# The order of all steps between up-projections given by tables per block, y summed by halves, decode scratch in other places

## The chip, the core and the metric

The kernel runs on one core of one Trainium2 chip. TensorE multiplies into PSUM banks, VectorE and ScalarE read those banks and work on SBUF, POOL (GpSimd) works on SBUF alone, and SyncE issues nearly all transfers. Each engine runs its own instructions strictly in the order of the program; between engines there are semaphores. The metric is the device time of the whole program in microseconds, as the median of several executions.

## What is computed

A Mamba2 scan over chunks (the kernel takes chunks of 128 tokens), and then a maxout feed-forward on its output:

```
# per batch b and head h, chunk by chunk (cum: running sum of log a in the chunk)
M       = (C @ B.T) * exp(cum_i - cum_j) * causal
y       = M @ x + (C @ state) * exp(cum_i)
state   = exp(cum_last) * state + sum_j B_j x_j exp(cum_last - cum_j)
...
# y as (3072 tokens, 256) = (batch * seq, heads * head_dim)
h   = max(y @ w1, y @ w2, y @ w3)          # 768 hidden values
out = h @ w_out                            # 256
```

The shapes are x (4, 8, 768, 32), B and C (4, 8, 768, 16), w1 to w3 (256, 768) and w_out (768, 256). The weights are float64 and are decoded in the kernel.

## The kernel before, in words

The sequence has six blocks of 128 tokens (NC = 6); one block holds 4 batches, so 512 tokens. Each block runs through the scan and then through the feed-forward, and the two are interleaved: while the feed-forward of block c runs on TensorE, the scan of block n = c + 1 is worked off between its matmuls.

The scan of a block n: B and C are transposed (`scan_b`, `scan_tc`), ScalarE masks C into even and odd heads (`scan_c`), E holds the decays (`scan_e` takes their exponential, `scan_cd` on VectorE multiplies them into C: Cd). `scores` makes four banks of scores for two batches, and four steps of `scan_weight` (L566) multiply them on VectorE with the decay matrix L, whose exponentials ScalarE makes in eight parts of four (`part`, `decay_part`, L459) after POOL has masked L (`decay_masks`, L452). `scan_old` multiplies the state with Cd (L581, four row groups of the array), `scan_own` adds the product of the weighted scores with x (L594); both sum into the two banks of y. `scan_y` makes of y its high part `hi` on ScalarE (L621), and `lo` and the difference `d` on VectorE (L622, L629). `scan_state` makes the state for the next block.

The feed-forward of a block c > 0 is a line of 18 units (nine weight matrices k, halves g): a unit opens a bank with two matmuls of `d` (`unit_open`, L699, the delta matmuls), ScalarE scales the bank by a constant (`down_scaled`, L685), four matmuls of the high and low parts follow (`unit`, L716), and VectorE copies the bank into m or takes the maximum (L721, L723). The banks of the units form a ring of four, and openings run up to three units ahead. Every third matrix completes a hidden row f: `hidden` makes its high part on ScalarE (L635) and then its low part and difference on VectorE (L638, L629). `down_next` issues the down product of a block in four pieces; L763 is that of block 0, L768 that of the others, where the pieces Y take the differences and X the other parts. `put` scales the result and sends it out.

Block 0 has plain float32 up-projections (18 steps n, L655), and in the steps between them the weights are decoded: ScalarE (L210, L219), VectorE (L211, L214), POOL (L220), and later a sign step on VectorE (L223). `split` then makes high part, low part and difference of each of the twelve weight chunks (step 0 on ScalarE, L257 and L258, steps 1 and 2 on POOL, L259 and L252). The seam between block 0 and block 1 sums y of block 1.

What stands between two units is given by lists per matrix (X1, Y1, D1, K1, W1 for block 1, X2, Y2, D2, K2 for the later ones), by `pop(2)` after each unit, which takes two steps off the list `later` (score weightings, `lo` and `d` of y, state), and by `after(1, ...)`, which puts the two parts of a hidden row one unit later each.

Of the kernel before, what the change touches and what calls it, by code (L numbers as in the profile page):

```python
# [20 lines left out]
def kernel(  # L21
# [53 lines left out]
    SMALL, LARGE = 2.0 ** -15, 122880.0 - 2.0 ** -7  # L75

# [114 lines left out]
    def decode_steps():  # L191
# [9 lines left out]
        room = six((1, 2, 5)[n % 3] if n < 10 else 2).rearrange("p (a f) -> p a f", a=2)  # L201
# [3 lines left out]
        def first():  # L205
# [3 lines left out]
            held["u"] = u = room[:, 0].bitcast(U32)  # L209
# [8 lines left out]
            r = room[:, 1].bitcast(U32)  # L218
# [23 lines left out]
    def weight_parts(k):  # L242
# [5 lines left out]

        def last():
            d = wsum.tile([P, 2, WCOL], F32R, tag="w", name="wd")  # L250
            parts[k].append(d)
            nc.gpsimd.tensor_tensor(  # L252
                out=d.rearrange("p k f -> p (k f)"), in0=hi.bitcast(FP32), in1=lo.bitcast(FP32),
                op=ALU.subtract)
# [4 lines left out]
            lambda: nc.gpsimd.tensor_tensor(  # L259
# [99 lines left out]
    Ls = {}  # L359
# [212 lines left out]
    def scan_old(c):  # L572

        st = blocks[c]
        st["y"] = ys = [att_bank([P, NB, P], "y") for _ in range(KD)]
        Sp = states[c]
        for b in range(NB):
            for r in range(NP):
                rows = slice(r * PN, (r + 1) * PN)
                q = r % 2 * 2 * D  # L580
                nc.tensor.matmul(  # L581
                    out=ys[r // 2][q:q + 2 * D, b],
                    lhsT=Sp[rows, b].rearrange("p g d -> p (g d)"), rhs=st["Cd"][rows, b],
                    start=(b == 0), stop=False, tile_position=(r * PN, q),
                    skip_group_check=True)

    def scan_own(c, bs):

        st = blocks[c]
        M = Ls[c]  # L590
        for b in bs:
            for h in range(NH):
                t, q = divmod(h, QH)
                nc.tensor.matmul(  # L594
                    out=st["y"][t][q * D:(q + 1) * D, b], lhsT=st["x"][:, b * NH + h],
                    rhs=M[:, b, h], start=False, stop=True,
                    tile_position=(0, q * D), skip_group_check=True)
# [17 lines left out]
    def scan_y(c):  # L615

        yT[c] = hi, lo, d = [
            six(3 * (c % 2) + j, F32R).rearrange("p (k t) -> p k t", k=KD) for j in range(3)]
        for t in range(KD):
            y = blocks[c]["y"][t].rearrange("p b i -> p (b i)")  # L620
            nc.scalar.activation(hi[:, t], y, AF.Copy, scale=HIGH)  # L621
            later.append(lambda t=t, y=y: nc.vector.tensor_tensor(  # L622
                out=lo[:, t], in0=y, in1=hi[:, t].bitcast(FP32), op=ALU.subtract))
            later.append(lambda t=t: difference(d[:, t], hi[:, t], lo[:, t]))
        later.append(lambda: ready.add(c))
# [41 lines left out]
    later, due = [], []  # L667
# [7 lines left out]
    def after(n, step):  # L675

        due.append((units[0] + n, step))

    def run_due():
        while due and due[0][0] <= units[0]:  # L680
            due.pop(0)[1]()
# [8 lines left out]
    AHEAD, ends = 2, []  # L690
# [13 lines left out]
    def unit():  # L704

        u = units[0]
        while len(opened) <= AHEAD and u + len(opened) < len(line) and (
                line[u + len(opened)][0] in ready):
            unit_open(u + len(opened))
        c, k, g = line[u]  # L710
        q, i = divmod(k, 3)
        o = opened.pop(u)
        cols = slice(g * P, (g + 1) * P)
        for kk in range(KD):
            for j in range(2):
                nc.tensor.matmul(  # L716
                    out=o, lhsT=weight_part(k, j, kk, cols), rhs=yT[c][j][:, kk],
                    start=False, stop=(kk == KD - 1 and j == 1), skip_group_check=True)
        if i == 0:
            m[g] = ffn.tile([P, BLK], FP32, tag="m", bufs=4, name="m")  # L720
            nc.vector.tensor_copy(out=m[g], in_=o)  # L721
        else:
            nc.vector.tensor_tensor(out=m[g], in0=m[g], in1=o, op=ALU.max)  # L723
        units[0] += 1
        run_due()
        if i == 2:
            last = c == NC - 1 and k == NW - 1

            def start(f=2 * q + g, src=m[g]):
                rest = hidden(f, src)  # L730
                if last:
                    rest()
                else:
                    after(1, rest)
            if last:
                if g == 1:
                    ends[0]()
                    start()
                else:
                    ends.append(start)  # L740
            else:
                after(1, start)
# [163 lines left out]
    signs, decodes = (0, 2, 3, 5, 7, 8, 10, 12, 14, 15, 17), (0, 2, 3, 5, 7, 8, 10, 12, 14, 15)  # L906
    W0 = {11: (0, 0), 12: (0, 1), 13: (0, 2, 1, 0), 14: (1, 1), 15: (1, 2, 2, 0), 16: (2, 1),
          17: (2, 2, 3, 0)}
    for n in range(NF * 3):
# [17 lines left out]
        if n in (13, 14, 16, 17):  # L927
            pop(2)
        if i == 0:
# [6 lines left out]
        if n in signs:  # L936
            sign()
        if n in decodes:
            decode()
        if n == 1:  # L940
            fj = from_last(R, a_sb, "fj")
        if n == 3:
# [8 lines left out]
            decay_masks(1, (0, 1))  # L951
        if n == 9:
            decay_masks(1, (2, 3))
        if n in (5, 7, 9, 11, 13, 14, 15, 16):
            part(1)
        if n == 11:
            transposed(1)
            scan_c(1)
            load(2, "C")
        if n == 12:  # L960
            scan_e(1)
            scan_cd(1)
            scores(1, 0)
        if n == 15:
            shared["att"] = False
            scores(1, 2)
        if n in W0:
            split(*W0[n])
    shared["ffn"] = False
    scan_old(1)  # L970
    scan_own(1, range(NB))
# [102 lines left out]
```

## Time and profile before

| | |
|---|---|
| time, median of 3 executions (lowest, highest) | 321.13 us (320.93, 323.64) |
| the profiled execution, whole | 320.5 us |
| its span (first to last instruction) | 318.8 us |
| mean granted clock of TensorE | 0.966 |
| busy: TensorE, VectorE, ScalarE, POOL | 279.9, 192.6, 181.9, 89.6 us |

Times in the profile are those of one execution and begin at the start of its span. "Idle before" is the time in which an engine waited before an instruction, and the name behind the arrow is what ended that wait. A granted clock of 1.00 is 2.4 GHz for TensorE, 0.5 is 1.2 GHz.

### The profile page before, as it was taken

What the parts mean: (1) busy time and instruction counts of PE and PEld (TensorE: products, weight loads), DVE (VectorE), ACT (ScalarE), POOL (GpSimd) and SP (SyncE); (2) the same over time, 40 slices, a digit from 0 to 9 for tenths busy, and PEclk for the clock granted to TensorE, in tenths of its full rate; (3) what the DMA queues carried; (4) which work ended last, traced back from release to release, by engine and by line L of the source; (5) the groups of instructions that cost most, each with busy time, mean ns of one, the idle gap of its engine ahead of it and who ended that gap; (6) DMA issues with size and microseconds to landing.
All of it is one profiled execution on the core that took longest, in us unless ns stands there. A gap on an engine that the chain in (4) does not pass through costs nothing.

```text
span 318.8 us, 5385 instructions
## 1 busy us (share of the span) xinstructions
PE 279.9 (88%) x2054; PEld 213.0 (67%) x2054; DVE 192.6 (60%) x296; ACT 181.9 (57%) x407; POOL 89.6 (28%) x84
## 2 busy tenths in 40 slices
PE   6899969599659978899997979997999997999993
PEld 4664434387438655688775868775898775797793
DVE  2767689762642468830888750888622967616662
ACT  2954977647943955923764833764844453425511
POOL 4344675759832670900021420021000000000000
PEclk9999999899957979979999999999999999999999
DMA  8979999898800359502708702800002000000001
GB/s 89 251 238 331 142 189 236 209 135 237 125 0 2 82 62 264 57 2 69 93 5 206 127 2 68 95 3 2 0 0 69 0 3 0 2 33 33 0 2 66
DMA packets 105049, 28.13 MB, mean 88 GB/s; under 512 B 75328, under 2 KB 101952, under 8 KB 105024
## 3 DMA queue, kind: packets, MB, share of 16 engines
q1 hardware_dynamic: 104720, 27.66, 42.7%
q8 instruction: 16, 0.26, 0.4%
q10 hardware_dynamic: 304, 0.13, 0.2%
q14 instruction: 9, 0.07, 0.1%
HBM read 24.54 MB, written 3.24 MB: 87 GB/s over the span
## 4 chain that ended last, share of the span: by engine, by line
PE 60%; DVE 23%; DMA 6%; ACT 4%; POOL 3%; issue 2%; SPq 0%; POOLq 0%; ACTq 0%
PE up L716 20%; PE up L699 11%; PE o L768 11%; PE s L558 5%; DVE h L629 4%; DVE h L638 4%; DMA raw_C<-in_C_dram 3%; DVE m L721 3%; PE o L763 3%; POOL six L220 3%; DVE w L223 2%; PE o L793 2%; PE y L594 2%; DMA rb<-in_moe_w_out_dram 2%; DVE six L629 2%
## 5 line engine op out<-in xcount | busy, mean ns | idle before, releaser
L716 PE MATMUL up<-six,wp 128*128 128x512 f32 x360 | 98.8, 398 | 0.0
L723 DVE TENSOR_TENSOR m<-m,up 128x512 f32<-128x512 f32 x60 | 40.9, 685 | 73.5 <-PE up L716 73.1
L685 ACT ACTIVATE up<-up 128x512 f32<-128x512 f32 x90 | 52.4, 584 | 55.9 <-PE up L699 48.6
L716 PEld LDWEIGHTS up<-six,wp 128*128 128x128 f32 x360 | 69.2, 192 | 15.5 <-ACT up L685 0.2
L699 PE MATMUL up<-six,wd 128*128 128x512 f32 x180 | 61.9, 424 | 8.0 <-DVE m L723 4.7
L459 ACT ACTIVATE L<-L,ncums 128x128 f32<-128x128 f32 x160 | 50.2, 391 | 0.9 <-POOL L L452 0.9
L699 PEld LDWEIGHTS up<-six,wd 128*128 128x128 f32 x180 | 31.6, 193 | 21.8 <-DVE m L723 7.9
L721 DVE COPY m<-up 128x512 f32<-128x512 f32 x30 | 20.6, 687 | 22.5 <-PE up L716 22.5
L566 DVE TENSOR_TENSOR L<-s,L 128x512 f32<-128x512 f32 x46 | 29.3, 682 | 0.7 <-ACT L L459 0.7
L655 PE MATMUL up<-six,w 128*128 128x512 f32 x64 | 28.8, 598 | 0.1
L558 PE MATMUL s<-six,six 32*128 32x256 f32 x192 | 20.9, 412 | 7.9 <-ACT six L500 4.0
L638 DVE TENSOR_TENSOR h<-m,h 128x512 fp32r<-128x512 f32 x30 | 26.0, 868 | 0.7 <-ACT h L635 0.7
L629 DVE SCALAR_TENSOR_TENSOR h<-h,h 128x512 fp32r<-128x512 f32 x30 | 25.4, 846 | 1.0
L452 POOL TENSOR_SCALAR_AFFINE_SELECT L<-L 128x1024 f32<-128x1024 f32 x20 | 25.4, 1292 | 0.0
L768 PE MATMUL o<-wp,h 128*128 128x256 f32 x192 | 24.3, 283 | 0.0
L768 PEld LDWEIGHTS o<-wp,h 128*128 128x128 f32 x192 | 23.9, 192 | 0.3
L558 PEld LDWEIGHTS s<-six,six 32*128 32x128 f32 x192 | 12.5, 184 | 15.3 <-ACT six L500 5.0
L545 POOL TENSOR_TENSOR S<-S,old 128x256 f32<-128x256 f32 x4 | 2.9, 734 | 69.7 <-DVE S L537 69.7
L220 POOL TENSOR_TENSOR six<-six 128x512 uint32<-128x512 uint32 x12 | 15.3, 1273 | 23.2 <-DVE six L214 16.1
L655 PEld LDWEIGHTS up<-six,w 128*128 128x128 f32 x64 | 11.8, 190 | 14.2 <-issue 11.1
L635 ACT ACTIVATE h<-m 128x512 fp32r<-128x512 f32 x30 | 18.7, 622 | 2.8 <-DVE m L723 2.7
L259 POOL TENSOR_TENSOR wp<-w,wp 128x512 fp32r<-128x512 f32 x12 | 15.4, 1284 | 15.5 <-ACT wp L257 15.5
(98 smaller groups left out, 326.2 us busy)
## 6 DMA issues: line engine op xcount, KB each, us to landing
L<-cums SPq DMA_DIRECT2D x10, 1024.0 KB, 8.8
rb<-in_moe_w_dram SPq DMA_DIRECT2D x9, 512.0 KB, 6.7
raw_x<-in_x_dram SPq DMA_DIRECT2D x6, 512.0 KB, 9.2
out_dram<-ob SPq DMA_DIRECT2D x10, 256.0 KB, 2.1
raw_B<-in_B_dram SPq DMA_DIRECT2D x6, 256.0 KB, 4.4
raw_C<-in_C_dram SPq DMA_DIRECT2D x6, 256.0 KB, 6.2
rb<-in_moe_w_out_dram SPq DMA_DIRECT2D x3, 512.0 KB, 4.8
E<-cums SPq DMA_DIRECT2D x40, 32.0 KB, 2.2
```

Of the source, the lines that this page charges most:

```text
L459: nc.scalar.activation(L[:, b, h], L[:, b, h], AF.Exp, bias=ncum[c][:, b * NH + h:b * NH + h + 1], scale=1.0)
L558: nc.tensor.matmul(out=s[:, i].rearrange("j g i -> j (g i)"), lhsT=st["BT"][rows, b], rhs=st["CT"][rows, :, b], start=(i == 0), stop=True, ...
L566: nc.vector.tensor_tensor(out=M, in0=s, in1=M, op=ALU.mult)
L629: nc.vector.scalar_tensor_tensor(out=out, in0=lo.bitcast(FP32), scalar=-1.0 / TAU, in1=hi.bitcast(FP32), op0=ALU.mult, op1=ALU.add)
L638: nc.vector.tensor_tensor(out=lo, in0=src, in1=hi.bitcast(FP32), op=ALU.subtract)
L655: nc.tensor.matmul(out=bank, lhsT=whole[3 * (f // 2) + i][:, k, f % 2 * P:(f % 2 + 1) * P], rhs=yT[0][:, k], start=(k == 0), stop=(k == KD ...
L685: nc.scalar.activation(bank, bank, AF.Copy, scale=-KAPPA)
L699: nc.tensor.matmul(out=o, lhsT=weight_part(k, 2, kk, cols), rhs=yT[c][2][:, kk], start=(kk == 0), stop=(kk == KD - 1), skip_group_check=True)
L716: nc.tensor.matmul(out=o, lhsT=weight_part(k, j, kk, cols), rhs=yT[c][j][:, kk], start=False, stop=(kk == KD - 1 and j == 1), skip_group_c ...
L721: nc.vector.tensor_copy(out=m[g], in_=o)
L723: nc.vector.tensor_tensor(out=m[g], in0=m[g], in1=o, op=ALU.max)
L768: nc.tensor.matmul(out=o[:, b % 2], lhsT=hs[f][p][:, tokens(b)], rhs=weight_part(NW + f // 2, p, f % 2, slice(0, DM)), start=(first and p ...
```

## The change

One table of words per block stage replaces the lists: FIRST for the 18 steps of block 0, SEAM and PRELUDE ahead of block 1, SECOND for block 1, STEADY for blocks 2 to 4, LAST for block 5; its entry i is worked off after unit i. A word is one step: `d` and `g` decode and sign, `w` a step of a weight split, `t`, `b`, `C`, `E`, `c`, `B`, `A` the steps of the scan, `s` scores, `x` the next step of `later`, `p` a part of the exponentials, `m` masks, `h` and `r` the first and second step of a hidden row, `y` the sum of y, `a` and `z` its `hi` and its `lo` with `d`, `D` a down product, `L` and `l` loads. Four things change besides the order: LATE says for which units the next opening comes behind the unit's matmuls and not ahead of them; COPIES puts some copies of m on ScalarE; WEIGHTS_DVE puts eleven of the 24 weight steps on VectorE and leaves the others on POOL; the sum of y does the old-state and own products of the first half (heads 0 to 3) and then those of the second. The scratch of the decodes moves from three `six` tiles into the places of the hidden rows.

```diff
+    COPIES = {c: (6, 7, 12,) if c == 1 else (1, 13,) for c in range(1, NC)}
+    LATE = {c: (2, 7, 11, 13, 15, 16, 17,) if c == 1 else (2, 6, 9, 13, 14, 16, 17,) for c in range(1, NC)}
+    WEIGHTS_DVE = ((0, 1), (2, 1), (2, 2), (3, 1), (4, 1), (5, 1), (5, 2), (6, 1), (6, 2), (9, 1), (11, 2),)
...
-        room = six((1, 2, 5)[n % 3] if n < 10 else 2).rearrange("p (a f) -> p a f", a=2)
+        r = n % 4
+        room = [hidden_place((2 * r + j) // 3, (2 * r + j) % 3, FP32) for j in range(2)]
...
+        def eng(step):
+            return nc.vector if (k, step) in WEIGHTS_DVE else nc.gpsimd
...
-    def scan_old(c):
+    def scan_own(c):
...
+        Sp, M = states[c], Ls[c]
+        for t, y in enumerate(ys):
+            for b in range(NB):
+                for r in range(2 * t, 2 * t + 2):
+                    rows = slice(r * PN, (r + 1) * PN)
+                    q = r % 2 * 2 * D
+                    nc.tensor.matmul(
+                        out=y[q:q + 2 * D, b],
+                        lhsT=Sp[rows, b].rearrange("p g d -> p (g d)"), rhs=st["Cd"][rows, b],
...
+            for b in range(NB):
+                for q in range(QH):
+                    h = t * QH + q
+                    nc.tensor.matmul(
+                        out=y[q * D:(q + 1) * D, b], lhsT=st["x"][:, b * NH + h],
+                        rhs=M[:, b, h], start=False, stop=True,
...
+        late = 2 * k + g in LATE[c]
...
+        opens(AHEAD if late else AHEAD + 1)
...
+        if late:
+            opens(AHEAD)
...
+    SEAM = "y A a a z z w3,1 x D"
+    PRELUDE = "w3,2 b B"
...
+        "m0,2 w5,2 p0 p0 r c s0 D x x x w8,0 w9,0 w7,1 h p0 w6,2 p0 D",
...
+        "r x p1 y a z a z p1 m1,2",
```

On ScalarE, at the first steps of block 0's feed-forward. The h_, six_ and rb names are decodes (two operations each); `m<-up` is the copy of a step's bank, L1071 after and L930 before; `fj` are factors that TensorE transposes after step 3. Before:

```order
L210 ACTIVATE six_350<-rb 128x512
L219 ACTIVATE six_350<-rb 128x512
L612 COPY six_343<-y 128x2x256
L930 COPY m<-up 128x512
L210 ACTIVATE six_388<-rb 128x512
L219 ACTIVATE six_388<-rb 128x512
L930 COPY m<-up 128x512
L335 ACTIVATE fj<-a_sb 96x128 x2
L210 ACTIVATE six_405<-rb 128x512
L219 ACTIVATE six_405<-rb 128x512
L210 ACTIVATE six_417<-rb 128x512
L219 ACTIVATE six_417<-rb 128x512
```

After, on the same engine at the same place:

```order
L616 COPY six_344<-y 128x2x256
L1071 COPY m<-up 128x512
L215 ACTIVATE h_1_390<-rb 128x512
L224 ACTIVATE h_2_391<-rb 128x512
L215 ACTIVATE h_0_398<-rb 128x512
L224 ACTIVATE h_1_399<-rb 128x512
L215 ACTIVATE h_0_408<-rb 128x512
L224 ACTIVATE h_1_409<-rb 128x512
L1071 COPY m<-up 128x512
L343 ACTIVATE fj<-a_sb 96x128 x2
```

The second copy of m and `fj` stand behind three decodes, where there was one.

On TensorE, at the seam: the last projection of block 0, y of block 1 (L581 and L590 are the old-state product, L594 and L598 the own product), the state product and the first down product. Before:

```order
L655 MATMUL up<-six_343,w 128x512 x4
L581 MATMUL y<-six_551,S 64x128 x16
L594 MATMUL y<-L,raw_x 32x128 x32
L526 MATMUL A<-raw_x,raw_B 32x64 x16
L763 MATMUL o<-w,h_0_457 128x256
```

After:

```order
L665 MATMUL up<-six_344,w 128x512 x2
L590 MATMUL y<-six_533,S 64x128 x8
L598 MATMUL y<-L,raw_x 32x128 x16
L590 MATMUL y<-six_533,S 64x128 x8
L598 MATMUL y<-L,raw_x 32x128 x16
L534 MATMUL A<-raw_x,raw_B 32x64 x16
L765 MATMUL o<-w,h_0_463 128x256
```

The old-state product of the second half has moved behind the own product of the first.

On VectorE, in block 1 around the first scores (L511 and L519 make the decayed C, L566 and L574 weight the scores, L267 and L260 are weight steps, L638, L629, L648 and L639 a hidden row). Before:

```order
L723 TENSOR_TENSOR m<-m,up 128x512 x4
L721 COPY m<-up 128x512
L638 TENSOR_TENSOR h_1_907<-m,h_0_906 128x512
L629 SCALAR_TENSOR_TENSOR h_2_908<-h_1_907,h_0_906 128x512
L511 TENSOR_TENSOR six_782<-trC,E 128x512
L721 COPY m<-up 128x512
L638 TENSOR_TENSOR h_1_933<-m,h_0_932 128x512
L629 SCALAR_TENSOR_TENSOR h_2_934<-h_1_933,h_0_932 128x512
L566 TENSOR_TENSOR L<-s,L 128x2x256 x2
```

After:

```order
L742 TENSOR_TENSOR m<-m,up 128x512 x4
L267 TENSOR_TENSOR wp<-w,wp 128x512 x2
L260 TENSOR_TENSOR wd<-wp 128x512
L648 TENSOR_TENSOR h_1_904<-m,h_0_903 128x512
L639 SCALAR_TENSOR_TENSOR h_2_905<-h_1_904,h_0_903 128x512
L519 TENSOR_TENSOR six_796<-trC,E 128x512
L574 TENSOR_TENSOR L<-s,L 128x2x256 x3
L260 TENSOR_TENSOR wd<-wp 128x512
```

Three weight steps stand ahead of the decayed C, and three weightings follow it at once, without the copy and the hidden row between.

## Rows read from the trace of the kernel before

**Rows 1.** Stretches of the span: length, then busy us and count by engine, clock, DMA.

```profile
26.56:69.58 43.02, 36.64 (x242) 20.00 (x241) 34.90 (x53) 28.36 (x66) 26.10 (x21) 0.96 1.01 205
69.58:124.40 54.82, 45.07 (x304) 33.62 (x302) 24.90 (x36) 37.38 (x90) 31.91 (x27) 0.88 0.52 102
124.40:173.79 49.39, 44.94 (x349) 35.96 (x349) 31.87 (x46) 29.14 (x70) 11.66 (x10) 0.97 0.41 75
173.79:221.62 47.83, 43.35 (x348) 34.75 (x348) 31.53 (x45) 28.11 (x66) 8.38 (x7) 1.00 0.34 60
221.62:266.64 45.02, 42.61 (x317) 34.23 (x317) 27.34 (x44) 23.71 (x50) 0.00 (x0) 1.00 0.04 13
266.64:305.00 38.36, 36.54 (x188) 30.35 (x189) 21.95 (x34) 15.78 (x28) 0.00 (x0) 1.00 0.04 15
```

The engines in a row are TensorE, its weight loads, VectorE, ScalarE and POOL.

**Rows 2.** TensorE's waits: who waited for whom, us in total, times, longest us.

```profile
PE o L768 <- DVE h L629: 5.0, 4, 2.0
PE up L699 <- DVE m L723: 4.7, 5, 1.3
PE s L558 <- ACT six L500: 4.0, 2, 2.6
PE y L581 <- DVE L L566: 3.8, 3, 3.5
PE s L558 <- DVE six L511: 3.6, 1, 3.6
PE up L699 <- DVE six L629: 3.3, 4, 0.8
PE o L763 <- DVE L L566: 2.8, 1, 2.8
```

**Rows 3.** Timeline at 24 to 27 us: start, us, instruction, idle time before it.

```profile
23.92 0.57 ACT L930 COPY m<-up 128x512 f32<-128x512 f32 x1
24.39 0.69 ACT L335 ACTIVATE fj<-a_sb 96x128 f32<-96x128 f32 x2
...
26.39 0.33 PE L343 MATMUL from_js_tp<-ident,fj 96*128 96x96 f32 x2
...
27.16 0.68 ACT L210 ACTIVATE six<-rb 128x512 f32<-128x512 f32 x1 [0.95 <-DMA rb<-in_moe_w_dram]
```

**Rows 4.** Timeline of TensorE: scores on two and on four row groups; y of block 4.

```profile
15.24 1.24 PE L558 MATMUL s<-six,six 32*128 32x256 f32 x8
...
46.21 1.15 PE L558 MATMUL s<-six,six 32*128 32x256 f32 x16 [2.62 <-ACT six L500]
...
213.02 1.10 PE L581 MATMUL y<-six,S 32*64 32x128 f32 x32
214.05 1.96 PE L594 MATMUL y<-L,raw_x 128*32 128x128 f32 x64
```

**Rows 5.** Timeline of TensorE: two down products of block 0.

```profile
66.53 2.86 PE L763 MATMUL o<-w,h 128*128 128x256 f32 x12
...
95.52 4.62 PE L763 MATMUL o<-w,h 128*128 128x256 f32 x12 [2.80 <-DVE L L566]
```

**Rows 6.** Timeline at 113 to 122 us, VectorE and POOL.

```profile
113.11 1.60 POOL L252 TENSOR_TENSOR wd<-wp 128x512 fp32r<-128x512 f32 x1
113.61 1.64 DVE L629 SCALAR_TENSOR_TENSOR h<-h,h 128x512 fp32r<-128x512 f32 x1
...
115.18 1.27 DVE L566 TENSOR_TENSOR L<-s,L 128x512 f32<-128x512 f32 x2
...
121.73 0.69 DVE L629 SCALAR_TENSOR_TENSOR h<-h,h 128x512 fp32r<-128x512 f32 x1
```

**Rows 7.** Timeline of TensorE: start of one unit's opening and of what follows the unit.

```profile
132.01 0.62 PE L699 MATMUL up<-six,wd 128*128 128x512 f32 x2
...
133.37 0.75 PE L768 MATMUL o<-wd,h 128*128 128x256 f32 x5
```

**Rows 8.** Groups of block 3 (173.79 to 221.62): busy us, mean ns, idle time before.

```profile
L558 PE MATMUL s<-six,six 32*128 32x256 f32 x32 | 4.0, 418 | 0.1
```

More of the change, by code (lines that the diff above doesn't have):

```diff
@@ L673, in pop, with take @@
             n -= 1
[L675 to L681, printed above, removed]
+    def take(steps):
+        if steps:
+            steps.pop(0)()
     def down_scaled(bank):
@@ L689 @@
     opened, m, ready = {}, {}, set()
-    AHEAD, ends = 2, []
+    AHEAD = 2
     def unit_open(u):
@@ L904, in scores, with act @@
             later.append(lambda r=r, s=s: scan_weight(n, b, r, s))
-    signs, decodes = (0, 2, 3, 5, 7, 8, 10, 12, 14, 15, 17), (0, 2, 3, 5, 7, 8, 10, 12, 14, 15)
-    W0 = {11: (0, 0), 12: (0, 1), 13: (0, 2, 1, 0), 14: (1, 1), 15: (1, 2, 2, 0), 16: (2, 1),
-          17: (2, 2, 3, 0)}
+    def act(word, c, n):
+        op, args = word[0], [int(i) for i in word[1:].split(",") if i]
+        at = n + args.pop(0) if op in "pm" else 0
+        if op == "p":
+            part(at)
+        elif op == "m" and at < NC:
+            decay_masks(at, (args[0], args[0] + 1))
+        elif op == "d":
+            decode()
+        elif op == "g":
+            sign()
+        elif op == "w":
+            split(*args)
+        elif op == "x":
+            take(later)
+        elif op == "h":
+            take(tops)
+        elif op == "r":
+            take(tails)
+        elif op == "a":
+            take(highs)
+        elif op == "z":
+            take(rests)
+            if not rests:
+                ready.add(n)
+        elif op == "D":
+            down_next()
+        elif n >= NC:
+            return
+        elif op == "b":
+            scan_b(n, att_bank)
+        elif op == "t":
+            scan_tc(n, att_bank)
+        elif op == "B" and n < NC - 1:
+            scan_bd(n)
+        elif op == "C":
+            scan_c(n)
+        elif op == "E":
+            scan_e(n)
+        elif op == "c":
+            scan_cd(n)
+        elif op == "s":
+            scores(n, args[0])
+        elif op == "A" and n < NC - 1:
+            later.append(scan_state(n, att_bank))
+        elif op == "y":
+            scan_own(n)
+            scan_y(n)
+        elif op == "L":
+            loads(c + 2)
+        elif op == "l":
+            later_loads(c + 2)
@@ new lines @@
+    STEADY = [
+        "t h E C b B c r",
+        "",
+        "A L h r x",
+        "l",
+        "s0 p0 x x",
+        "m1,0",
+        "",
+        "p0 D x D x",
+        "D D h",
+        "r",
+        "h r s2 x x p1 h",
+        "p0 h",
+        "x",
+        "r x p1 y a z a z p1 m1,2",
+        "",
+        "p1 p1",
+        "r",
+        "",
+    ]
+    LAST = [
+        "h",
+        "",
+        "",
+        "h r",
+        "r",
+        "",
+        "D",
+        "",
+        "D D D h",
+        "",
+        "r h",
+        "r",
+        "h",
+        "h",
+        "r r",
+        "",
+        "",
+        "h r",
+    ]
```

216 lines of the change are left out of this document (79 added, 137 removed).

## The prediction

> **What bounds the kernel now.** I cut the span into stages: 26.56 is the end of the fourth up-projection of block 0, the later cuts are the first delta matmuls of a block. In each stage TensorE is busy 82 to 95% of the time, VectorE, ScalarE and POOL far less, so TensorE's order of work sets the time. Two things can be won: its idle time (6.4, 9.8, 4.5, 4.5, 2.4 and 1.8 us, 29.3 in all) and what it loses at 1.2 GHz instead of 2.4, where the granted clock of a stage is under 1 [rows 1]. The list of TensorE's waits tells what ends the idle time: nearly always a step that stands late in another engine's queue. Scores wait for the masked C or the decayed C, y and the down product of block 0 for banks or factors that the score weighting on VectorE gives, the delta matmuls of the next block for its y, the down product for the last hidden row [rows 2]. In block 3 VectorE has 31.5 us of work and ScalarE 28.1 in 47.8 us [rows 1], so an order without these waits can exist.
>
> **The change, part by part.** Base: TensorE's busy time of a stage, plus the idle time I expect to be left.
>
> *26.56 to 69.58 (rest of block 0, y of block 1).* Gone is the 2.6 us wait of the scores for the masked C [rows 2]: B of block 1 is turned three steps earlier, and C is masked two steps before the scores. New: the table puts the decodes of weights 2, 3 and 4 all into step 0. Today ScalarE has its copy of m and its `fj` done when it comes to decode 4, and waits for the data of it until 27.16 [rows 3]. After the change the copy for step 1 and `fj` stand behind that decode: 27.16, two operations of 0.68 that follow each other at 0.6, 28.4; then the copy (24.39 − 23.92 = 0.5) and `fj` (0.7): 29.6. TensorE comes to the transposes of `fj` at 26.39 [rows 3] and waits, some 3 us. (Bounds: 0 if the load lands 3 us sooner, but its place in SyncE's queue is the same; 4 if the projection before it is held too.) y of block 1 waits 3.5 us today [rows 2], as the last weighting hangs on the last exponentials. In halves, heads 0 to 3 need only two of the four last weightings; but two weight splits now stand ahead of the last exponentials. Between 0 and 3.5 is left; I take 1.9, the middle. The clock of the stage is 0.96: (1 − 0.96) × 2 × 43 = 3.4 us at half, 1.7 lost [rows 1]. With 1.0 for the halves (below): 36.6 − 1.7 + 1.0 + 3.0 + 1.9 = 40.8 if the clock stays up, 42.5 if it falls again; I take 41.0, **−2.0**. The decodes' four scratch places instead of three free decode 11 of waiting for its place; its data come late, so I give it nothing.
>
> *y by halves, in all five y.* The 32 records of the old-state product took 1.10 us, the 64 of the own product 1.96 [rows 4]. The old product runs its four row groups (r = 0 to 3) side by side. A half has two of them. That pairs are no faster than fours per step, scores show: 8 records on two row groups took 1.24 us, 16 records on four 1.15 [rows 4]. So a half of the old product takes as long as the whole: +0.9, and two more switches between the kinds, +0.1. **+1.0 us of TensorE a block**, hidden by nothing as TensorE is the bound (bounds: 0 if pairs went twice as fast, 1.3). The Trainium skill (TensorEngine Tiling (Array Packing), section Tiling Modes, Key Properties) says that changing the tiling mode drains TensorE, which speaks against halves; with it the two added switches would cost somewhat over 0.1. What halves buy is in the stages below: ScalarE makes `hi` of the first half while TensorE sums the second.
>
> *69.58 to 124.40 (block 1).* Busy 45.07 at clock 0.88: (1 − 0.88) × 2 × 54.8 = 13.2 us at half, 2.8 of it the down product's wait, half of the other 10.4 lost: 5.2 [rows 1, 2]. What half clock does, the down records show: 12 took 4.62 us after that wait, 2.86 in the seam [rows 5]. The waits are 3.6 (scores), 2.8 (down), y's, and 1.3 at the next opening [rows 2]. In the table E and the masked C stand three windows before the scores. Between unit 5 and the scores VectorE has three weight steps, a hidden row (two operations) and the decayed C: six of about 0.69, 4.2 us [rows 6]. TensorE has a down product, two units and two openings in that time, 2.86 + 12 × 0.227 = 5.6 [rows 5, 7]: no wait, with 1.4 to spare. The down product behind the scores needs a bank that their first weighting frees, which can only follow them: 0.8 left. At y two hidden rows stand around the fourth weighting: 0.8 left. 45.07 − 5.2 + 1.0 + 1.6 = 42.5, **−12.3**. This also holds seven of the eleven weight steps that VectorE takes over from POOL, 0.69 to 1.64 us each [rows 6], 5 to 11 us on an engine that has 24.9; and three copies of m that go to ScalarE, 0.57 each [rows 3], which has 37.4 of 54.8 [rows 1]. All of that lies beside TensorE's 42 us in the sum.
>
> *124.40 to 266.64 (blocks 2 to 4).* Today's waits: 1.3 and 0.8 us at each opening, 2.0 for the hidden row in two of the blocks [rows 2]. The two score products of block 3 took 4.0 us, as they wait for banks among their records [rows 8], against 2 × 1.15 where they are free [rows 4]: −1.7. Opening: after y come three units and two openings, 16 matmuls at 0.227 ((133.37 − 132.01) / 6 [rows 7]), 3.6 us. Behind the end of y stand `hi` of the second half (0.6) and its `lo` and `d` (1.4), 2.0; today it is two `hi`, four of VectorE's and three maxima, over 5. So the delta of the next block is ready. Hidden row: `h` and `r` stand in the first three windows, the product that needs it behind unit 7. Busy 44.94, 43.35, 42.61 [rows 1]; less 1.4 for the clock in block 2 (0.97: 3.0 us at half) and 1.7 each for the scores, plus 1.0 each for the halves and 0.5 each left idle: 43.3, 43.2, 42.4, together 128.9 against 142.2: **−13.3**.
>
> *266.64 to 305.0 (block 5).* Busy 36.54 [rows 1], 0.3 left idle: **−1.5**. The tail keeps its order.
>
> Sum: 318.8 − 2.0 − 12.3 − 13.3 − 1.5 = 289.7 us of span. The profiled execution had 320.5 us around 318.8, 1.7 more, and the median is 321.13, 0.6 above that: 292.0. I take **292**.
>
> **The rivals.** (A) *VectorE becomes the bound in block 1.* With POOL busy beside it an operation of VectorE between SBUF places took 1.64 us instead of 0.69, while the weighting, which reads PSUM, kept its pace of 0.6 [rows 6]. Block 1 has eight hidden-row operations, seven weight steps and two deltas of y of that kind; 0.9 more on half of them is 8, and VectorE has 24.9 + 5 + 8 = 38 us in 42. Where it falls behind, y and the down product wait as today: 6 to 9 us, **300**. Against it: POOL loses the eleven steps. The Trainium skill (GPSIMD Engine Reference, section Key points) says that GpSimd shares its SBUF interfaces with VectorE when VectorE's instruction has two SBUF inputs; each weight step that moves is such a one, and the 1.64 us agree with that. (B) *The halves buy nothing*: `lo` and `d` of the second half stand behind other VectorE work, and the openings still wait 2.1 in four blocks, 8.4: **300**. For it: VectorE works strictly in order. (C) *Slower.* In the tables `r` (VectorE) often stands in the same or the next window as the `h` (ScalarE) that it needs; before, a unit lay between. If ScalarE is late, VectorE stands, the maxima behind do not free their banks, and TensorE stops at an opening. A stop is worth about the 1.3 us of today's opening wait [rows 2]; it decides from six such stops in each of five blocks, 39 us, against the 29 won, at **331**. For it: ScalarE has exponentials of 1.2 us a part in between. Against: it is free a third of each block [rows 1]. (D) *The waits only move*, as the new one at `fj`: within 1%, **320**.
>
> **How the numbers follow.** Forecast 0.66, A 0.16, B 0.09, D 0.04, C 0.05. Low end: the idle time that I left in blocks 1 to 4 is not there (−3.1), y of block 1 does not wait (−1.9), the halves cost 0.4 a block and not 1.0 (−3): 284. High end: A or B with the clock falling in the first stage and a block's slack used up (300 + 1.5 + 2.5): 304. One per cent (3.2 us) is about what this kernel's runs can tell from no change. Faster 0.91 (forecast, A, B), same 0.04 (D), slower 0.05 (C).
>
> **What would show it.** After the change: a TensorE wait of about 3 us before the `fj` transposes near 26.5, none of more than 1 us at block 1's scores; block 1 from its first delta to that of block 2 in 42 to 43 us at a clock over 0.95; blocks 2 to 4 with 42 to 43.5 us each and no wait for a `d` at the opening; the old product of y as two stretches of about 1 us. I am wrong if TensorE's waits in blocks 2 to 4 stay over 2 us a block, if weight steps on VectorE average over 1.2 us and y of block 2 waits for them (A), or if half clock stays.

## The result, and the profile after

The changed kernel takes 283.26 us (median of 4 executions, 282.33 to 283.49), the kernel before 321.06 us in the same comparison (320.93 to 323.64): a ratio of 0.880, with a 95% interval of 0.875 to 0.885. Here and below, executions that took over 1.5% longer than the fastest of the same kernel, at a lower granted clock, are left out of times and ratios. Faster was forecast, but 292.0, and the time lies 0.7 us below the low end of the range, 284. The profiled execution of 282.33 us has a span of 280.6 us and a granted clock of 0.999. What lies before the first cut of the stages and behind the last one differs by 0.1 us each from the kernel before (26.47 and 13.7 us), so the gain lies in the six stages between.

The page of the changed kernel, busy time of each engine:

```profile
PE 266.0 (95%) x2054; PEld 208.4 (74%) x2054; DVE 184.1 (66%) x296; ACT 185.8 (66%) x418; POOL 72.4 (26%) x73
```

TensorE's waits in the changed kernel (who waited for whom, us in total, times, longest):

```profile
PE from_js_tp L351 <- ACT fj L343: 2.5, 1, 2.5
PE spread L380 <- POOL mask L317: 2.5, 1, 2.5
PE s L566 <- ACT six L508: 1.4, 1, 1.4
PE up L665 <- ACT m L1071: 0.9, 1, 0.9
PE y L590 <- DVE L L574: 0.9, 1, 0.9
PE up L657 <- ACT six L616: 0.7, 1, 0.7
PE o L765 <- DVE L L574: 0.6, 1, 0.6
PE up L706 <- ACT m L738: 0.2, 1, 0.2
```

The rows for the scores of block 1, for the last hidden row and for the openings [rows 2] are gone but for 0.2 us. Of the two score waits for the masked C [rows 2] the one of 2.6 us is gone; the one of 1.4, at 12 us, is left. New are the wait for `fj`, as forecast (2.5 for "some 3"), and 0.9 us for a copy of m in block 0. y of block 1 waits 0.9 us instead of 3.5, the down product of block 0 0.6 instead of 2.8.

The stages of the changed kernel, cut as in [rows 1] (the last cut is the start of block 5's down product, L795):

```profile
26.47:66.71 40.24, 35.92 (x243) 19.32 (x243) 35.26 (x57) 29.58 (x69) 23.10 (x18) 1.00 1.00 212
66.71:106.30 39.59, 38.98 (x301) 31.07 (x300) 27.08 (x41) 36.78 (x89) 21.39 (x19) 1.00 0.66 118
106.30:149.75 43.45, 43.22 (x356) 35.81 (x354) 27.54 (x44) 30.92 (x77) 9.84 (x10) 1.00 0.52 102
149.75:191.55 41.80, 41.80 (x350) 34.68 (x348) 26.97 (x42) 28.81 (x70) 6.60 (x7) 1.00 0.43 78
191.55:232.69 41.14, 41.14 (x317) 34.19 (x316) 26.55 (x41) 24.84 (x54) 0.00 (x0) 1.00 0.04 14
232.69:266.89 34.20, 34.20 (x186) 29.58 (x184) 19.05 (x30) 16.56 (x30) 0.00 (x0) 1.00 0.05 16
```

Length minus TensorE's busy time is 4.3, 0.6, 0.2, 0, 0 and 0 us, where [rows 1] gave 6.4, 9.8, 4.5, 4.5, 2.4 and 1.8. The clock is 1.00 in every stage; it was 0.88 in block 1. The puzzle is in the busy column: with about as many records it fell too, by 1.5 us in blocks 3 and 4 each and 2.3 in block 5, although y takes longer than before. The forecast had 0.7 of it in blocks 3 and 4 (1.7 less for the scores, 1.0 more for the halves) and nothing in block 5. A y of the changed kernel, on TensorE's timeline, against [rows 4]:

```profile
141.91 1.09 PE L590 MATMUL y<-six,S 32*64 32x128 f32 x16
142.93 1.08 PE L598 MATMUL y<-L,raw_x 128*32 128x128 f32 x32
143.94 1.09 PE L590 MATMUL y<-six,S 32*64 32x128 f32 x16
144.96 1.08 PE L598 MATMUL y<-L,raw_x 128*32 128x128 f32 x32
145.97 1.20 PE L728 MATMUL up<-six,wp 128*128 128x512 f32 x4
```

From start to start this is 145.97 − 141.91 = 4.06 us. Half of the old-state product (16 records, 1.02 us to the next row) takes as long as all of it did (214.05 − 213.02 = 1.03).

### The profile page after: what moved, and what is told of

Read it like the earlier page. It is cut to its first block, busy times and chain, and to the rows that moved or that the text cites. A ratio compares the mean times of both kernels' runs of the same rounds, so it can differ in the third digit from the quotient of the medians.

```text
span 280.6 us, 5395 instructions
## 1 busy us (share of the span) xinstructions
PE 266.0 (95%) x2054; PEld 208.4 (74%) x2054; DVE 184.1 (66%) x296; ACT 185.8 (66%) x418; POOL 72.4 (26%) x73
## 4 chain that ended last, share of the span: by engine, by line
PE 77%; DMA 9%; ACT 7%; DVE 2%; issue 2%; POOL 1%; SPq 0%; ACTq 0%; POOLq 0%
PE up L728 27%; PE up L706 14%; PE o L770 12%; DMA rb<-in_moe_w_dram 5%; PE o L765 4%; PE y L590 4%; PE y L598 4%; PE s L566 3%; PE o L795 3%; PE up L665 2%; ACT L L467 2%; DMA cums<-a_sb 2%; DMA rb<-in_moe_w_out_dram 1%; PE spread L396 1%; ACT up L692 1%
## 5 line engine op out<-in xcount | busy, mean ns | idle before, releaser
L728 PE MATMUL up<-six,wp 128*128 128x512 f32 x360 | 94.0, 392 | 0.0
L706 PE MATMUL up<-six,wd 128*128 128x512 f32 x180 | 54.5, 402 | 0.2 <-ACT m L738 0.2
L574 DVE TENSOR_TENSOR L<-s,L 128x512 f32<-128x512 f32 x46 | 29.6, 681 | 2.6 <-PE s L566 1.7
L460 POOL TENSOR_SCALAR_AFFINE_SELECT L<-L 128x1024 f32<-128x1024 f32 x20 | 22.6, 1160 | 0.0
L225 POOL TENSOR_TENSOR h<-h,h 128x512 uint32<-128x512 uint32 x12 | 16.5, 1372 | 20.1 <-DVE h L219 13.1
L639 DVE SCALAR_TENSOR_TENSOR h<-h,h 128x512 fp32r<-128x512 f32 x30 | 20.8, 692 | 1.0
L648 DVE TENSOR_TENSOR h<-m,h 128x512 fp32r<-128x512 f32 x30 | 20.9, 696 | 0.5 <-ACT h L645 0.4
L740 DVE COPY m<-up 128x512 f32<-128x512 f32 x19 | 13.1, 690 | 11.5 <-PE up L728 11.2
L783 ACT ACTIVATE ob<-o 128x512 f32<-128x512 f32 x10 | 6.0, 596 | 21.2 <-PE o L770 14.7
L566 PE MATMUL s<-six,six 32*128 32x256 f32 x192 | 15.3, 399 | 1.4 <-ACT six L508 1.4
L566 PEld LDWEIGHTS s<-six,six 32*128 32x128 f32 x192 | 10.1, 184 | 6.5 <-issue 3.6
L228 DVE SCALAR_TENSOR_TENSOR w<-rb,h 128x512 uint32<-128x512 uint32 x12 | 10.2, 849 | 4.5 <-POOL h L225 4.4
```

Source lines behind the costliest of these rows:

```text
L460: nc.gpsimd.affine_select(out=Ls[c][:, b], in_=Ls[c][:, b], pattern=[[0, NH], [1, P]], compare_op=ALU.is_ge, fill=MASKED, base=0, channel_ ...
L566: nc.tensor.matmul(out=s[:, i].rearrange("j g i -> j (g i)"), lhsT=st["BT"][rows, b], rhs=st["CT"][rows, :, b], start=(i == 0), stop=True, ...
L574: nc.vector.tensor_tensor(out=M, in0=s, in1=M, op=ALU.mult)
L639: nc.vector.scalar_tensor_tensor(out=out, in0=lo.bitcast(FP32), scalar=-1.0 / TAU, in1=hi.bitcast(FP32), op0=ALU.mult, op1=ALU.add)
L648: nc.vector.tensor_tensor(out=lo, in0=src, in1=hi.bitcast(FP32), op=ALU.subtract)
L706: nc.tensor.matmul(out=o, lhsT=weight_part(k, 2, kk, cols), rhs=yT[c][2][:, kk], start=(kk == 0), stop=(kk == KD - 1), skip_group_check=True)
```

## The experiments

The two theories at the start. One: TensorE is the bound, the gain is its waits, and the halves of y only cost (about 1.1 us in each of five blocks), since the new order alone frees the openings. The other, on which the forecast stood: the halves are what lets `hi` of the next block begin early and so takes the opening waits away. All runs are given as a ratio to the kernel before on the same chip, which ran 320.4 to 325.5 us there. The new places of the decodes' scratch are in every run of the new order; what they are worth was not measured. The start of the program differs between executions of one kernel, with the landing of its first loads and what follows from it: y of block 1 began at 59.15 us in one execution of the changed kernel and at 61.78 in another. So each profiled execution is also compared by its stretch from the first matmul of y of block 1 to the first of block 5's down product: 305.01 − 60.98 = 244.0 us in the kernel before, 266.89 − 59.15 = 207.7 in the changed one.

**y in one piece, order as after.** The changed kernel with the old-state product of both halves first and then the own products:

```diff
+        for b in range(NB):
+            for r in range(NP):
...
+                    out=ys[r // 2][q:q + 2 * D, b],
...
         for t, y in enumerate(ys):
-            for b in range(NB):
-                for r in range(2 * t, 2 * t + 2):
...
             for b in range(NB):
                 for q in range(QH):
```

> The kernel after, with the old-state product of both halves of y ahead of the own product, as before; all else as after. Theory (the order between the units made the gain, the halves cost TensorE time): the old product takes 1.1 us once instead of twice, 1.1 to 1.2 us less in each of five y; behind y the opening needs hi 0.6, hi 0.5 and four VectorE operations of 0.68, 3.9 us, against 3.8 us of units, so an opening waits 0 to 0.5: 277.5 to 280.5 us. Rival (the halves are what frees the openings): the openings wait about 2 us again in four blocks, 286 to 288 us.

Measured: 282.8 us, ratio 0.876 (0.866 to 0.885); the profiled execution had 278.7 us of span. No opening waits. The stretch from y of block 1 took 265.01 − 62.47 = 202.5 us, 5.2 less than in the changed kernel, five times 1.04. The start of the program hid most of that in the median, which lies above the 277.5 to 280.5 that I had expected: `fj` waited 3.9 us instead of 2.5, and half clock followed at 30.9 for 3.4 us. So it was repeated beside the changed kernel itself.

**The changed kernel again, as it is**, on the chip of the next two runs.

> The kernel after, unchanged, as the reference for the runs of this call: 282 to 284 us, with the fj wait of 2 to 4 us by the time at which the fifth weight chunk lands in this run.

Measured: 283.06 us, ratio 0.879 (0.870 to 0.888); its `fj` wait was 3.2 us this time, and the stretch 207.8.

**y in one piece, again** (the same edit):

> The kernel of e1_y_whole again, beside the kernel after on the same chip. Theory: from the first y to the last down product 5.2 us shorter than after (202.5 against 207.7, as in the first run of it), and the time 3.5 to 5.2 us under that of the kernel after in this call. Rival (what the halves cost comes back in the seam, where y waits for its banks): within 1 us of it.

Measured: 279.25 us, ratio 0.865 (0.850 to 0.879), 3.8 us under the changed kernel on the same chip, with much the same start (`fj` waits 3.5); the stretch is 202.5 again. It is faster than both kernels. The stretches from each y to the next, of this kernel:

```profile
62.25:102.33 40.08, 39.30 (x337) 31.80 (x337) 28.22 (x43) 32.99 (x80) 24.43 (x22) 1.00 0.74 139
102.33:143.28 40.95, 40.84 (x354) 33.82 (x348) 27.27 (x45) 29.66 (x71) 9.87 (x10) 1.00 0.57 104
143.28:183.95 40.67, 40.67 (x350) 33.91 (x349) 26.80 (x44) 28.80 (x68) 6.61 (x7) 1.00 0.51 98
183.95:223.93 39.98, 39.98 (x318) 33.42 (x317) 26.39 (x43) 27.74 (x64) 0.00 (x0) 1.00 0.04 14
```

The last two are 1.1 us shorter than the same stretches of the changed kernel (183.71 − 141.91 = 41.80, and 41.14), and nothing waits at the openings. In this order the halves buy nothing.

**The halves alone, in the kernel before.** `scan_old` does the two halves, `scan_own` nothing, all else as before:

```diff
+        for t, y in enumerate(ys):
+            for b in range(NB):
+                for r in range(2 * t, 2 * t + 2):
...
     def scan_own(c, bs):
...
+        pass
```

> The kernel before, with y by halves alone. Theory: five times 1.1 us more on TensorE, and the openings, where today 2.1 us are waited, win back up to 1.5 in four blocks because the first half's low part is ready earlier: 319 to 326 us. Rival (the halves make the gain): openings without a wait, 315 us or less.

Measured: 327.96 us, ratio 1.019 (1.005 to 1.034): slower by about 6 us (2 to 11 by the interval), where five times 1.1 are 5.5, and above the 326 at which my range ended. Four openings still wait, up to 1.3 us for m and 0.8 for the difference. (Only the places of the waits are taken from its profile.) The halves neither remove those waits nor pay for themselves in the old order either.

**The decode of the third early weight a step later**, where it does not stand ahead of `fj`:

```diff
-        "g d d g g d",
-        "",
+        "g d d g g",
+        "d",
```

> The kernel after, with the third decode of step 0 moved to step 1, behind fj on ScalarE. Theory: the 2.5 us wait before the transposes of fj goes, but the seam hangs on the last decodes, whose data land at a fixed time, so the waits at steps 13 to 17 and at y of block 1 (0.9 and 0.9 now) grow: 0 to 1.5 us faster, 281.8 to 283.3. Rival (TensorE's order is all): the whole 2.5 us, 280.8.

Measured: 282.86 us, ratio 0.877 (0.867 to 0.887), about the time of the changed kernel, which did not run on that chip. The wait for `fj` is gone, and in its place TensorE waits as follows (waits of this kernel):

```profile
PE up L665 <- ACT m L1071: 1.6, 1, 1.6
PE up L665 <- DVE m L1075: 1.2, 1, 1.2
PE y L590 <- DVE L L574: 1.2, 1, 1.2
...
PE up L665 <- DVE w L228: 0.6, 1, 0.6
```

That is 4.6 us for 4.3 in the changed kernel, and y of block 1 starts at 59.71 instead of 59.15. The stall at `fj` was real and was where the forecast put it, but against that execution nothing is won by taking it away: waits of the same sum come up behind the decodes. In both the load had landed early: the decode that needs it begins at 27.39 us here and at 26.92 in the changed kernel. In the run of y in one piece on the same chip, with the decode in its old place, it began at 28.48, half clock followed, and y of block 1 started 2.8 us later than here (62.47). Whether the later decode keeps that when the load lands late, no run shows.

**All weight steps on POOL**, with the order of after:

```diff
-    WEIGHTS_DVE = ((0, 1), (2, 1), (2, 2), (3, 1), ... (11, 2),)
+    WEIGHTS_DVE = ()
```

> The kernel after, with all weight steps on POOL again. Theory (the order, not the engine): POOL has 21 us of work in block 1's 39.6 and gets seven steps of 1.3 us, 30 us, VectorE loses as many of 0.7: block 1 longer by 0 to 2 us, 283 to 285.5. Rival (the shift of engine is a large part of the gain): parts of weights come late for the openings, block 1 longer by 4 us or more, 287 and up.

Measured: 284.84 us, from a single execution. The stretch, which lies behind the start, took 209.1 us, 1.4 more than the changed kernel. Repeated:

> The kernel of e3_weights_pool again, beside the kernel after on the same chip. Theory: block 1 (y to y) 1.3 us longer, as in the first run of it, and the time 1 to 3 us over that of the kernel after in this call. Rival: the shift of the weight steps is worth 5 us or more.

Measured: 284.71 us, ratio 0.883 (0.874 to 0.893), 1.7 us over the changed kernel on the same chip. The stretch is 209.1 again. Block 1 from y to y takes 42.05 us instead of 40.69; the other blocks differ by less than 0.1. The eleven steps on VectorE are worth 1.4 us in that block. There the second operation of its first two hidden rows, which takes 0.69 us in the changed kernel, now stands beside POOL's work:

```profile
81.85 1.46 DVE L639 SCALAR_TENSOR_TENSOR h<-h,h 128x512 fp32r<-128x512 f32 x1
...
93.97 1.67 DVE L639 SCALAR_TENSOR_TENSOR h<-h,h 128x512 fp32r<-128x512 f32 x1
```

**The tables alone**: y in one piece, and neither weight steps on VectorE, nor copies on ScalarE, nor late openings:

```diff
-    COPIES = {c: (6, 7, 12,) if c == 1 else (1, 13,) for c in range(1, NC)}
-    LATE = {c: (2, 7, 11, 13, 15, 16, 17,) if c == 1 else (2, 6, 9, 13, 14, 16, 17,) for c in range(1, NC)}
-    WEIGHTS_DVE = ((0, 1), (2, 1), (2, 2), (3, 1), ... (11, 2),)
+    COPIES = {c: () for c in range(1, NC)}
+    LATE = {c: () for c in range(1, NC)}
+    WEIGHTS_DVE = ()
```

> The tables alone: the kernel after with y whole, all weight steps on POOL, all copies of m on VectorE and no late openings (openings three ahead, ahead of the unit's matmuls, as before). Theory (the order is nearly all of the gain): 280 to 288 us. Rival (late openings or copies carry a large part): over 295 us, with waits of the delta matmuls for VectorE's maxima of 0.3 us and more at many units.

Measured: 298.51 us, ratio 0.926 (0.918 to 0.934). So my expectation failed: of the 13.5% that order and placement give together (ratio 0.865), the tables alone give 7.4, a little over half; its stretch is 219.5, 17.0 more than 202.5. (Its start has 6.8 us at half clock, so the stretches compare better: the tables alone shorten it by 24.5 of 41.5 us.) TensorE's waits of this kernel:

```profile
PE s L566 <- DVE six L519: 3.8, 1, 3.8
PE up L706 <- DVE m L742: 2.7, 4, 1.3
...
PE up L706 <- DVE m L740: 2.1, 4, 1.0
```

The scores of block 1 wait for the decayed C again, and the openings for VectorE. In the seam, y waits 1.6 us, 0.1 more than with all three edits, and here half clock follows, 3.4 us of it, half of that lost in block 1. Its blocks 1 and 4, from y to y:

```profile
63.81:112.13 48.32, 44.27 (x337) 35.29 (x337) 25.79 (x36) 32.41 (x78) 36.22 (x31) 0.89 0.55 100
...
198.12:240.56 42.44, 40.96 (x317) 33.39 (x316) 27.68 (x43) 26.78 (x62) 0.00 (x0) 1.00 0.04 14
```

Block 4 is 2.5 us longer than with all three edits (39.98), and only 1.5 of that shows as idle time. The other 1.0 is counted as busy, though the matmuls are the same. The next run shows where it sits.

**No late openings**: y in one piece, LATE empty, the rest as after.

```diff
-    LATE = {c: (2, 7, 11, 13, 15, 16, 17,) if c == 1 else (2, 6, 9, 13, 14, 16, 17,) for c in range(1, NC)}
+    LATE = {c: () for c in range(1, NC)}
```

> The kernel with y whole (e6), and no late openings: each opening is three units ahead, ahead of the unit's own matmuls. Of the 18.8 us between e8 and e6, theory one (the place of the openings is the large part: an opening ahead of the unit needs the bank of the unit before it, whose maximum VectorE has only just begun): 8 us or more over e6, 288 us and up, and in blocks 2 to 4 periods of 42 us and more with little idle time shown. Rival (the weight steps and copies are the large part, VectorE's or POOL's load): under 284 us.

Measured: 284.7 us, ratio 0.878 (0.869 to 0.888), about 5 us over y in one piece, between the two that I had expected (8 or more over it, and under 284); the stretch, behind the start, is 208.9, 6.3 more. From y to y it took 40.03, 42.82, 41.93 and 41.29 us, so 0, 1.9, 1.3 and 1.3 more than with late openings. TensorE's timeline of this kernel before y of block 5:

```profile
227.88 1.07 PE L728 MATMUL up<-six,wp 128*128 128x512 f32 x4
229.39 0.73 PE L706 MATMUL up<-six,wd 128*128 128x512 f32 x2 [0.44 <-DVE m L742]
229.96 1.09 PE L728 MATMUL up<-six,wp 128*128 128x512 f32 x4
230.98 1.10 PE L589 MATMUL y<-six,S 32*64 32x128 f32 x32
```

Four matmuls at 0.227 us from 227.88 would let the next start at 228.79. It starts at 229.39, 0.60 later, and the row shows 0.44: records of these matmuls are 0.39 us long on average where they follow each other at 0.227, so the modelled end of the one before covers 0.16 us of a wait. The same in the kernel before, at the first openings of block 4:

```profile
219.24 1.07 PE L716 MATMUL up<-six,wp 128*128 128x512 f32 x4
221.62 0.50 PE L699 MATMUL up<-six,wd 128*128 128x512 f32 x1 [1.31 <-DVE m L723]
222.95 0.50 PE L699 MATMUL up<-six,wd 128*128 128x512 f32 x1 [0.82 <-DVE six L629]
```

The first wait cost 221.62 − 220.15 = 1.47 us for 1.31 shown; the second, behind a single matmul, 222.95 − 221.85 = 1.10 for 0.82. Busy time of TensorE holds these parts.

**No copies on ScalarE**: y in one piece, COPIES empty, the rest as after.

```diff
-    COPIES = {c: (6, 7, 12,) if c == 1 else (1, 13,) for c in range(1, NC)}
+    COPIES = {c: () for c in range(1, NC)}
```

> The kernel with y whole (e6), and all copies of m on VectorE. Theory (VectorE has 27 of 40 us in a block): 0 to 2 us over e6, 279 to 282. Rival (VectorE's queue at units 1, 13 and 6, 7, 12 is what the openings wait for): 4 us or more, 284 and up.

Measured: 288.71 us, ratio 0.891 (0.884 to 0.899), about 9 us over y in one piece, where I had expected 0 to 2. The stretch is 214.3, 11.8 more, and 8.1 of that is in block 1 (48.18 us from y to y instead of 40.08), of which 1.5 is a wait for `raw_C` that no other run of the new order shows. So it is some 7 us there and 3.4 in blocks 2 to 4, where openings wait for VectorE. The copies were costed at nothing but ScalarE's time; what they are worth stands on VectorE's queue. Its timeline in this kernel before the decayed C (L519):

```profile
82.39 0.69 DVE L740 COPY m<-up 128x512 f32<-128x512 f32 x1 [1.07 <-PE up L728]
83.32 0.69 DVE L740 COPY m<-up 128x512 f32<-128x512 f32 x1 [0.23 <-PE up L728]
83.93 1.14 DVE L260 TENSOR_TENSOR wd<-wp 128x512 fp32r<-128x512 f32 x1
84.99 1.75 DVE L648 TENSOR_TENSOR h<-m,h 128x512 fp32r<-128x512 f32 x1
86.77 1.46 DVE L639 SCALAR_TENSOR_TENSOR h<-h,h 128x512 fp32r<-128x512 f32 x1
88.16 0.68 DVE L519 TENSOR_TENSOR six<-trC,E 128x512 f32<-128x512 f32 x1
```

The two copies wait for their units, the weight step and the hidden row behind them come 4.4 us later than in the changed kernel (below) and then take 1.14, 1.75 and 1.46 us, and the scores on TensorE wait. Of the 4.4 us 1.7 were there before the copies (the weight step ahead of them begins at 80.64 for 78.96), from the start and the wait for `raw_C`; but the tables alone, without copies on ScalarE and without that wait, show 3.8 us at the scores as well.

```profile
88.89 2.07 PE L566 MATMUL s<-six,six 32*128 32x256 f32 x10 [4.51 <-DVE six L519]
```

The granted clock shows half from 87.3 to 94.1. In the changed kernel VectorE does the same operations with nothing to wait for:

```profile
78.96 0.69 DVE L267 TENSOR_TENSOR wp<-w,wp 128x512 fp32r<-128x512 f32 x1 [0.94 <-ACT wp L265]
79.57 0.69 DVE L260 TENSOR_TENSOR wd<-wp 128x512 fp32r<-128x512 f32 x1
80.17 0.68 DVE L648 TENSOR_TENSOR h<-m,h 128x512 fp32r<-128x512 f32 x1
80.89 0.69 DVE L639 SCALAR_TENSOR_TENSOR h<-h,h 128x512 fp32r<-128x512 f32 x1
81.50 0.68 DVE L519 TENSOR_TENSOR six<-trC,E 128x512 f32<-128x512 f32 x1
```

Taken out one at a time, the three placements cost the stretch 6.3 us (late openings), 11.8 or, less the wait for `raw_C`, 10.3 (copies) and 1.4 (weight steps, taken out with y by halves), together 18.0 to 19.5; taken out together, 17.0.

**Two attempts on what is left at the seam.** y in one piece; in the last two steps of block 0 the last decode stands behind two score weightings, and two weight splits behind the weightings and the exponentials; the second run has the decode a step later as well.

```diff
-        "s2 d w1,2 w2,0 x w3,0 x",
-        "p0 x x w2,1 g w2,2",
+        "s2 w1,2 x x d p0",
+        "x x w2,0 w3,0 w2,1 g w2,2",
```

> The kernel with y whole (e6), and the last two rows of the table for block 0 put in another order: two weightings ahead of the last decode on VectorE, the last exponentials ahead of two weight splits on ScalarE. Theory (the 1.5 us wait of y in the seam is a place in a queue): the wait goes, 1 to 2 us under e6. Rival (the seam hangs on the time at which the last weight chunk lands): the splits and the first openings come later by as much, within 0.7 us of e6.

> e11, and the third decode of step 0 moved to step 1 as in e2. Theory: the 2.5 to 3.5 us wait at fj goes, and since the waits of the seam no longer stand behind the late decodes, 1 to 2.5 us of it stay won against e11. Rival: it comes back at the steps of block 0 that wait for ScalarE's copies, as in e2, within 0.7 us of e11.

Measured: 278.60 us, ratio 0.860 (0.853 to 0.867), and 279.00 us, 0.858 (0.849 to 0.868): both within 0.7 us of y in one piece, whose 279.25 came from another chip; the stretch is 203.0 in both, 0.5 more than without these edits. So my theory failed: y of block 1 waits 1.46 us in the first, as without the edit. VectorE's timeline shows what came in the place of the decode that stood ahead of the weightings (0.8 us):

```profile
57.06 1.74 DVE L228 SCALAR_TENSOR_TENSOR w<-rb,h 128x512 uint32<-128x512 uint32 x1 [0.29 <-POOL h L225]
...
59.32 1.27 DVE L574 TENSOR_TENSOR L<-s,L 128x512 f32<-128x512 f32 x2
```

The sign step ahead of them, which waits for POOL, now takes 1.74 us with a weight step of POOL beside it (56.98 to 58.25); with y in one piece it took 0.69. In the second run the `fj` wait is gone and 0.6, 1.2 and 2.2 us return in block 0, as in the run above with the later decode. What the start of y would be without that sign step ahead was not tried; the wait is 0.9 to 1.5 us.

## Why the prediction was wrong, point by point

The waits went where the forecast put them, and no rival's time came. The size failed, and two beliefs were wrong without costing the sum: that the halves free the openings, and that the copies on ScalarE are worth nothing. That the waits of block 1 came as forecast is luck in that part, since the copies were in the change but not in the reasoning.

**The step that failed: the base, "TensorE's busy time of a stage, plus the idle time I expect to be left".** Forecast and measured length of the six stages: 41.0 and 40.24; 42.5 and 39.59; 43.3 and 43.45; 43.2 and 41.80; 42.4 and 41.14; 36.8 and 34.20. Together 8.8 us; with 0.2 outside the stages, rounded, that is 289.7 against 280.6 of span. (The cuts have moved by a few matmuls: block 1's stage has 301 records for 304 [rows 1], block 2's 356 for 349, block 5's 186 for 188. Seven at 0.227 are 1.6, so block 2 too was some 1.4 too long.) Of the 8.8, idle time is 3.1: I left 4.9, 1.6, 0.5, 0.5, 0.5 and 0.3, and 4.3, 0.6, 0.2 and nothing are there. The halves cost 0.15 a block more than I took. So about 6.4 us was work in my sum that is none: 8.8 − 3.1 + 0.7. It is about 1 us in each of blocks 3 and 4, and more in blocks 1 and 5.

What stands in its place: busy time holds a part of every wait. Shown are 1.47 for 1.31, 1.10 for 0.82 and 0.60 for 0.44, so a wait shorter than about 0.16 us behind such a matmul would not be shown at all. The Trainium skill (TensorE: Matmul & The Clock Gate, section Single matmul latency) gives a single bf16 matmul a constant of 166 ns beyond its columns at the high clock; the 0.16 us of two of these three, with float32 operands, agree. Three kernels with y in one piece and 317 or 318 records bear it out over a whole block 4, y to y. With all edits it takes 39.98 us without idle time. The tables alone take 42.44 with 1.5 idle, so 1.0 is hidden. The kernel before took 45.01 (from 213.02 to 258.03) with 2.4 idle, so 2.6 is hidden, of which I had found 1.7 in the scores by their mean [rows 8] and missed 0.9. In block 5 the kernel before ran at full clock [rows 1], so the 1.9 us hidden there (38.36 − 34.20, less 1.8 shown as idle and 0.45 for two records) are no half clock; how the part in block 1 divides among waits and half clock was not measured. A base of records times their cadence would have erred the other way. For block 4 from y to y the kernel before gives 108 × 0.227 for the up-projections [rows 7], 72 × 0.120 for the down products, 2.2 for the scores, 0.8 for the transposes and 2.9 for y, 39.0 in all (worked out afterwards). That is 1.0 under the 39.98 measured without waits; the busy time of 42.6 is 2.6 over it, 0.9 with the 1.7 taken off for the scores. The cadence leaves out the switches between kinds of matmul: two up-projections behind y took 0.58 us to the next row there (215.93 to 216.51), two in a line of their own 0.45 (217.43 to 217.88).

**The range.** Its low end held the idle time and the halves at their best, but no error of the base. I had taken the waits of [rows 2] at the lengths shown.

**26.56 to 69.58.** Forecast 41.0, measured 40.24. `fj` waits 2.5 us (3.0), y 0.9 (1.9), a copy of m that I had not named 0.9. The clock stayed up. The stall's size rests on when a load lands: in the runs that keep that place for the decode `fj` waited 0.5 to 3.9 us.

**y by halves.** Forecast +1.0 a block, measured 4.06 − 2.91 = 1.15, where 2.91 is 233.89 − 230.98 with y in one piece. The old-state half takes as long as the whole: +1.01. The own product went from 1.88 to 2.02, two more switches: +0.14 where I had 0.1. The Trainium skill (TensorEngine Tiling (Array Packing), section Tiling Modes, Key Properties) says that a change of the tiling mode drains the array, and the 0.14 us agree with its sign. What the halves were to buy was wrong: with y in one piece the openings wait for nothing. The three units between y and the deltas, 3.6 us in my own working, cover the chain behind y, 2.0 by that working and one `hi` of 0.6 more without halves; in that run y of block 5 ends at 226.84, its last difference at 229.48, and the first delta matmul starts at 230.60.

**Block 1.** Forecast 42.5, measured 39.59, the largest miss of a stage. The waits are where I put them: none at the scores, 0.6 at the down product (0.8), none at y of block 2 (0.8). I took it for an effect of the order. The tables without the copies and late openings show that it is not: they take 48.32 us from y to y, with 3.8 us at the scores and 1.7 lost to half clock in the seam. I had given the copies no worth, and those of block 1 carry some 7 us.

**Blocks 2 to 4 and 5.** Of each half microsecond that I left, 0.2 was there in block 2 and nothing in the others, and the scores are free, as I had it. The rest is the base.

**The rivals.** (A) did not come: VectorE is busy 27.1 us in block 1, not 38. Its eleven weight steps have medians of 0.68 and 0.69 us, with one of 1.55 and one of 1.43, and the two operations of a hidden row fell from 0.87 and 0.85 us on average to 0.70 and 0.69. With all weight steps on POOL these averages are 0.70 and 0.75, but they run over the whole program, and the weight steps end before 114 us. In block 1 the second operation took 1.46 and 1.67 us with the weight steps on POOL and 0.69 without, so there the steps that POOL loses keep VectorE free, as I had it. From y of block 2 to that of block 3 the two averaged 1.02 and 1.03 us before, and 0.68 and 0.69 with the weight steps in either place: there it is the order. Its mechanism is real, as the run without copies shows: VectorE behind by a few operations met POOL's, and two operations took 1.75 and 1.46 us. (B) is half right: the halves buy nothing, but the openings do not wait. (C) and (D) are not seen over the whole; (D) describes the seam alone, where the stall at `fj` moves to copies of m and back.

## What to carry to other kernels

Where one engine is the bound, sum its work from start to start in stretches without waits, the switches between kinds of matmul among them, and not as its busy time: a wait begins under the modelled end of the record before it, and a block can be shorter than its busy time says. An order that frees the bound engine depends on the queues of the others, so take each placement apart (here three copies on another engine were worth some 7 us of a block, mostly through one operation that came earlier). And ask of each edit that adds work to the bound engine whether the wait it is to remove is still there without it.

## What the runs showed of the hardware

- A wait of 3.8 to 4.5 us on TensorE at the scores of block 1 came with 6.8 us at half clock (92.8 to 99.6 with the tables alone, 87.3 to 94.1 without copies), and waits of 3.2 to 3.9 us for `fj` were followed by 3.4 us of it; the wait of 2.5 us for `fj` in the changed kernel was not. The length of the wait alone does not tell: in the kernel before, a wait of 2.0 us for a hidden row that ended at 136.16 was followed by half clock from 136.7 to 140.1, and with the tables alone one of 1.6 us before y that ended at 63.81 by half clock from 65.5 to 68.9, while 1.5 us at that place with y in one piece was not.
- Two row groups at 32 x 64 did not go faster per step than four: 16 records on two groups took 1.09 us, 32 records on four 1.10.
- The decode that waits for the same load at the start began at 26.92 us in the changed kernel and at 28.48 with y in one piece, and the wait for `fj` behind it was 2.5 and 3.9 us.
